# A retention layer with a token-mixing layer behind it: one product for wq and wk, explicit PSUM banks, late weights, a new order, 512-byte pieces and at most three loads on their way

## Chip, cores and metric

One core of one Trainium2 chip. The metric is the device time of the kernel in microseconds (us). A profile's span (first to last instruction) is 1.7 us shorter than the time of the same run. Runs of one kernel scatter: on the day of the experiments the kernel before ran from 108.9 to 118.0 us (on three chips), with the granted TensorE clock of a run between 0.92 and 0.98. A run counts as fast when it is within 1.5% of the fastest run of the same kernel.

## The reference, cut to what matters

```python
# retention: a recurrent state per batch and head, S = 768 steps, 8 heads of 64
state = gamma * state + outer(k[t], v[t]);   y[t] = scale * q[t] @ state
# token mixing on x = y of all heads side by side (4 batches x 768 x 512)
wq = x @ w_q;  wk = x @ w_k                              # 512 -> 64
W_tok = scale * einsum('bsd,btd->bst', wq, wk)
mixed = einsum('bst,btd->bsd', W_tok, x)
out = relu(mixed) @ w_out
```

The kernel works in 12 "pairs" of 256 tokens, three per batch. A pair needs 0.5 MB each of q, k and v. `mixed` is computed as wq times (wk^T x), so the mixing of a batch starts when its three pairs are through.

## The kernel before

Every instruction has its place in a hand-made list, `ORDER`: a token such as `sc.3.1` or `ekT.4:A` emits one step of one pair, the letter naming the engine (A ScalarE, V VectorE, P GpSimd). The engines work through their own instructions in that order.

```python
STAGES = 6
at_psum = pool("at_psum", 1, space=PSUM)   # scores: 2 banks, one buffer
y_psum  = pool("y_psum", 1, space=PSUM)    # 2 banks
s_psum  = pool("s_psum", 1, space=PSUM)    # 1 bank
psum    = pool("psum", 3, space=PSUM)      # everything else: 3 banks in turn

for p in range(STAGES):
    for name in "kqv":
        load(name, p)                      # k of pair 0 on ScalarE's queue, the rest on SyncE's
    if p == 2:                             # weights ahead of pair 3
        nc.sync.dma_start(out=wq_stage, in_=moe_w_q.rearrange("(a p) h -> p a h", p=128))
        nc.sync.dma_start(out=wk_stage, in_=moe_w_k.rearrange("(a p) h -> p a h", p=128))
        nc.sync.dma_start(out=wout_stage, in_=moe_w_out.rearrange("(a p) m -> p a m", p=128))
...
def wqk(e, p):                             # wq x transposed (wq doubled), wk x not
    for a in range(NDM):
        matmul(out=ps[:, 0:256], lhsT=wq_sb[:, a], rhs=xT[:, a])            # 4 of 256 columns
    for c in range(2):
        for a in range(NDM):
            matmul(out=ps[:, 256 + c*64 : ...], lhsT=xT[:, a, c], rhs=wk_sb[:, a])  # 8 of 64
def ew(e, p): copy(e, st["wqk"], st["wqk_ps"])                              # one copy of 384 columns
...
nc.sync.dma_start(out=dst, in_=pairs[p]["o"])                               # 4 KB a row
```
(cut and shortened to the parts that matter here)

Of the kernel before, what the change touches and what calls it, by code (L numbers as in the profile page):

```python
# [15 lines left out]

ORDER = """
fill.80 ck.0:V trk.0 cq.0:V ekT.0:A trq.0 cv.0:V fill.2 eqT.0:V
st.0 es.0.0:A sc.0.0 X.0 eat.0.0:V es.0.1:A sc.0.1 ck.1:P ia.0.0
eat.0.1:V cq.1:P Y.0 trk.1 fill.6 ekT.1:A ia.0.1 ex.0:V cv.1:P  # L20
trq.1 eqT.1:A xt.0 st.1 sc.1.0 exT.0:V ck.2:P es.1.0:A eat.1.0:V
X.1 es.1.1:A sc.1.1 cq.2:P trk.2 eat.1.1:V ia.1.0 ekT.2:V Y.1
ia.1.1 cv.2:A ex.1:V trq.2 st.2 fill.4 eqT.2:V xt.1 es.2.0:A
W:V sc.2.0 exT.1:A X.2 wqk.0 eat.2.0:V wqk.1 WO:A ew.0:V
sc.2.1 ew.1:V ia.2.0 eat.2.1:V ck.3:P Y.2 ia.2.1 ex.2:A cq.3:P
trk.3 xt.2 ekT.3:A fill.4 exT.2:V cv.3:A wqk.2 trq.3 ew.2:A
st.3 eqT.3:V zm.0 ck.4:P es.3.0:A ez.0:A X.3 sc.3.0 es.3.1:A
mx.0 eat.3.0:V r.0.1:A cq.4:P trk.4 r.0.0:A sc.3.1 ekT.4:A ia.3.0
eat.3.1:V mx.1 Y.3 r.1.0:A pj.0.0 cv.4:P r.1.1:A trq.4 fill.4
eo.0.0:A st.4 eqT.4:V ia.3.1 ck.5:P pj.0.1 ex.3:A es.4.0:V sc.4.0  # L30
eo.0.1:A X.4 eat.4.0:V xt.3 es.4.1:V cq.5:P trk.5 ekT.5:A exT.3:V
pj.1.0 sc.4.1 eo.1.0:A cv.5:P trq.5 eat.4.1:V ia.4.0 mx.2 eqT.5:A
YS.4 ia.4.1 es.5.0:A ck.6:P r.2.0:A ex.4:V wqk.3 trk.6 r.2.1:A
sc.5.0 pj.1.1 ew.3:A eat.5.0:V cq.6:P eo.1.1:A X.5 ekT.6:V ia.5.0
sc.5.1 cv.6:A xt.4 eat.5.1:V trq.6 pj.2.0 exT.4:A eqT.6:V ck.7:P
YS.5 eo.2.0:A sc.6.0 es.6.0:A ia.5.1 eat.6.0:V wqk.4 cq.7:P ex.5:A
pj.2.1 ew.4:A trk.7 eo.2.1:V xt.5 ekT.7:V sc.6.1 X.6 exT.5:V
cv.7:A eat.6.1:V trq.7 ia.6.0 eqT.7:A wqk.5 ck.8:P es.6.1:A sc.7.0
ew.5:V YS.6 eat.7.0:V es.7.0:A ia.6.1 zm.1 ex.6:A cq.8:P sc.7.1
ez.1:V X.7 eat.7.1:V trk.8 es.7.1:A xt.6 ekT.8:V cv.8:A ia.7.0  # L40
trq.8 exT.6:V Y.7 st.8 eqT.8:V mx.3 es.8.0:A ia.7.1 ck.9:P
r.3.1:A r.3.0:V sc.8.0 ex.7:V wqk.6 eat.8.0:V pj.3.0 ew.6:A cq.9:P
trk.9 eo.3.0:A pj.3.1 ekT.9:V X.8 eo.3.1:A cv.9:P mx.4 sc.8.1
r.4.0:A r.4.1:V trq.9 eat.8.1:V pj.4.0 eqT.9:A ck.10:P ia.8.0 eo.4.0:V
mx.5 YS.8 r.5.1:A r.5.0:V sc.9.0 ia.8.1 es.9.0:V pj.4.1 cq.10:P
ex.8:V trk.10 eo.4.1:A eat.9.0:V pj.5.0 ekT.10:A trq.10 cv.10:A eo.5.0:V
sc.9.1 X.9 eat.9.1:V ia.9.0 xt.8 ck.11:P xt.7 eqT.10:A exT.7:V
pj.5.1 exT.8:V wqk.7 es.9.1:V cq.11:P eo.5.1:A trk.11 ew.7:A wqk.8
YS.9 ew.8:V cv.11:P ekT.11:A sc.10.0 ia.9.1 es.10.0:A eat.10.0:V trq.11
ex.9:A zm.2 eqT.11:V X.10 ez.2:A sc.10.1 es.10.1:A ia.10.0 eat.10.1:V  # L50
mx.6 YS.10 r.6.0:A xt.9 es.11.0:A r.6.1:A sc.11.0 exT.9:V ia.10.1
mx.7 eat.11.0:V pj.6.0 r.7.0:A ex.10:V r.7.1:A wqk.9 eo.6.0:A pj.6.1
ew.9:A X.11 eo.6.1:A sc.11.1 ia.11.0 eat.11.1:V mx.8 pj.7.0 r.8.0:A
r.8.1:A Y.11 eo.7.0:V ia.11.1 pj.7.1 ex.11:A eo.7.1:A xt.10 xt.11
exT.10:V pj.8.0 exT.11:V wqk.10 eo.8.0:A wqk.11 ew.10:A pj.8.1 ew.11:A
zm.3 eo.8.1:A ez.3:A mx.9 r.9.0:A r.9.1:V mx.10 pj.9.0 r.10.1:A
r.10.0:V eo.9.0:V pj.9.1 mx.11 eo.9.1:A r.11.1:V r.11.0:A pj.10.0 eo.10.0:A
pj.10.1 eo.10.1:A pj.11.0 eo.11.0:A pj.11.1 eo.11.1:A
""".split()

STAGES = 6
# [3 lines left out]
def kernel(  # L65
# [10 lines left out]




# [3 lines left out]
    nc = tc.nc  # L83
# [20 lines left out]

# [3 lines left out]
    ost_pool = pool("ost", 7)  # L108
# [8 lines left out]
    moe_pool = pool("moe", 6)  # L117
    relu_pool = pool("relu", 2)
    PSUM = bass.MemoryType.PSUM
    at_psum = pool("at_psum", 1, space=PSUM)  # L120
    y_psum = pool("y_psum", 1, space=PSUM)
    s_psum = pool("s_psum", 1, space=PSUM)
    psum = pool("psum", 3, space=PSUM)

    pairs = [dict() for _ in range(NG)]
    state_ps = [None] * B
# [13 lines left out]
    def load(name, p):  # L140
        src = {"k": k, "q": q, "v": v}[name]
        b, cp = divmod(p, NP)
        t = stage_pool.tile([128, H, 2, D], FP32, name=name + "_st")
        eng = nc.scalar if (name, p) == ("k", 0) else nc.sync
        eng.dma_start(
            out=t.rearrange("g h j d -> g h (j d)"),
            in_=src[b, :, cp * 2 * C : (cp + 1) * 2 * C, :].rearrange(
                "h (g j) d -> g h (j d)", j=2
            ),
        )  # L150
        pairs[p][name + "_st"] = t

    wq_stage = wstage_pool.tile([128, NDM, DH], FP32, name="wq_stage")
    wk_stage = wstage_pool.tile([128, NDM, DH], FP32, name="wk_stage")
    wout_stage = wstage_pool.tile([128, NDM, DM], FP32, name="wout_stage")
    for p in range(STAGES):
        for name in "kqv":
            load(name, p)
        if p == 2:
            nc.sync.dma_start(out=wq_stage, in_=moe_w_q.rearrange("(a p) h -> p a h", p=128))  # L160
            nc.sync.dma_start(out=wk_stage, in_=moe_w_k.rearrange("(a p) h -> p a h", p=128))
            nc.sync.dma_start(
                out=wout_stage, in_=moe_w_out.rearrange("(a p) m -> p a m", p=128)
            )

    def release(name, p):

        if p + STAGES < NG:
            load(name, p + STAGES)



    warm = const_pool.tile([128, 128], BF16, name="warm")
# [23 lines left out]

# [20 lines left out]
    wq_sb = const_pool.tile([128, NDM, 2, DH], BF16, name="wq_sb")  # L218
    wk_sb = const_pool.tile([128, NDM, DH], BF16, name="wk_sb")
    wout_sb = const_pool.tile([128, NDM, DM], BF16, name="wout_sb")  # L220

    def W(e):
        copy(
            e,
            wq_sb,
            wq_stage[:, :, None, :].to_broadcast([128, NDM, 2, DH]),
        )
        if e == "A":
            nc.scalar.mul(out=wk_sb, in_=wk_stage, mul=float(wk_scale))
        else:  # L230
            ENGINES[e].tensor_scalar_mul(out=wk_sb, in0=wk_stage, scalar1=float(wk_scale))
# [4 lines left out]


    fills = [0]

    def filled(dst):  # L240
        for i in range(fills[0]):
            if dst.dtype == BF16:
                nc.tensor.transpose(dst, warm, identity)  # L243
            else:
                nc.tensor.matmul(out=dst, lhsT=warm, rhs=warm, start=True, stop=True)
        fills[0] = 0
# [3 lines left out]
    def decay(e, p, name, table):  # L250
        st = pairs[p]
        st[name + "s"] = cast_pool.tile([128, HP, 2, 2, D], BF16, name=name + "s")
        ENGINES[e].tensor_tensor(  # L253
            out=st[name + "s"].rearrange("p hp j x d -> p x (hp j) d"),
            in0=st[name + "_st"].rearrange("p (x hp) j d -> p x (hp j) d", x=2),
            in1=table[:, p % NP]
            .rearrange("p (x hp) j -> p x (hp j)", x=2)
            .to_broadcast([128, 2, HP * 2, D]),
            op=ALU.mult,
        )  # L260
        release(name, p)

    def ck(e, p):
        decay(e, p, "k", fk)

    def cq(e, p):
        decay(e, p, "q", fq)

    def cv(e, p):
        st = pairs[p]  # L270
        st["vs"] = cast_pool.tile([128, HP, 2, 2, D], BF16, name="vs")
        copy(
            e,
            st["vs"].rearrange("p hp j x d -> p x (hp j) d"),
            st["v_st"].rearrange("p (x hp) j d -> p x (hp j) d", x=2),
        )
        release("v", p)

    def trk(e, p):
        st = pairs[p]  # L280
        ps = psum.tile([128, HP, 2, 2, G], BF16, name="ktr_ps", tag="ps")
        filled(ps[:, 0, 0].rearrange("p c g -> p (c g)"))
        for hp in range(HP):
            for j in range(2):
                nc.tensor.transpose(ps[:, hp, j], st["ks"][:, hp, j], identity)  # L285
        st["ktr_ps"] = ps

    def ekT(e, p):
        st = pairs[p]
        st["kT"] = qkt_pool.tile([128, HP, 2, 2, G], BF16, name="kT")  # L290
        copy(e, st["kT"], st["ktr_ps"])

    def trq(e, p):
        st = pairs[p]
        ps = psum.tile([128, HP, 2, 2, G], BF16, name="qtr_ps", tag="ps")
        filled(ps[:, 0, 0].rearrange("p c g -> p (c g)"))
        for hp in range(HP):
            for j in range(2):
                nc.tensor.transpose(ps[:, hp, :, j, :], st["qs"][:, hp, j], identity)  # L299
        st["qtr_ps"] = ps  # L300

    def eqT(e, p):
        st = pairs[p]
        st["qT"] = qkt_pool.tile([128, HP, 2, C], BF16, name="qT")
        copy(e, st["qT"], st["qtr_ps"].rearrange("p hp c j g -> p hp c (j g)"))

    def sc(e, p, half):
        st = pairs[p]
        ps = at_psum.tile([128, 2, 2, 2, C], FP32, name="at_ps", tag="at")
        filled(ps[:, 0, 0, 0, :])  # L310
# [13 lines left out]
        st["at_ps", half] = ps  # L324

    def eat(e, p, half):
        st = pairs[p]
        st["at", half] = at_pool.tile([128, 2, 2, 2, C], BF16, name=f"at_sb{half}")
        st["eat", half] = ENGINES[e].tensor_tensor(  # L329
# [283 lines left out]
```

## Time and profile before

| | before |
|---|---|
| time, median | 112.4 us |
| span in the profile | 109.7 us |
| first useful TensorE instruction | 8.9 us |
| last matmul ends | 105.2 us |
| last load issued | 61.5 us |
| TensorE / VectorE / ScalarE / GpSimd busy | 93.8 / 64.9 / 60.0 / 49.4 us |

TensorE runs the matmuls and transposes, and is the busiest engine. The prediction below shows the slices, the stretches and the waits. To compare kernels I use one more number, the **work done** by a moment: the matmuls of every group that started before it, times their warm spacing (0.056 us a transpose or a 128-column product, 0.216 a 512-column projection and so on, from the chain and the fills). It counts neither fills (dummy matmuls, explained below) nor waits. Some matmul records are missing in a trace, so totals are 75 to 78 us; differences under 1 us mean nothing. It is to be compared only with itself: the prediction adds up whole groups and has 16.2 us by 36.1 us for the kernel before, this count has 14.9 by 36.

### The profile page before, as it was taken

Reading aid. Unit: us, or ns where it says so; the run is one execution under the profiler, and the core shown is the slowest. Engines: PE = TensorE matmul, PEld = TensorE weight load, DVE = VectorE, ACT = ScalarE, POOL = GpSimd, SP = SyncE. Lnnn points to the kernel's source line nnn. Section 1 sums busy time; section 2 is a strip of 40 time slices with the busy share of each in tenths; the row PEclk is TensorE's granted clock in tenths of the full one; section 3 lists DMA queues with packets and bytes.
Section 4 is the critical chain, followed back from the end, with each engine's and each line's share of the span. In section 5 each row is a group of like instructions: output and inputs, shape, how many; then the busy total and the mean of one; then the engine's idle time right before and its main releaser. Section 6 shows DMA issues by size and latency. Waiting matters only on the chain.

```text
span 109.7 us, 4707 instructions
## 1 busy us (share of the span) xinstructions
PE 93.8 (85%) x2132; PEld 68.9 (63%) x2132; DVE 64.9 (59%) x87; ACT 60.0 (55%) x94; POOL 49.4 (45%) x41
## 2 busy tenths in 40 slices
PE   3999596994579899999998959999999999958930
PEld 3998485783458576667687837557787647633400
DVE  1066756894422665687688849799857954225100
ACT  5004137265273975958848515549587866554640
POOL 6405968008699996968229999321000000000000
PEclk9999958999967999999999999999999999999999
DMA  1999999999999999999999999824040022430471
GB/s 38 309 347 346 342 342 238 313 334 306 289 327 337 345 344 304 339 337 333 287 297 281 300 354 370 332 115 166 31 197 0 6 87 111 191 158 33 191 312 73
DMA packets 40917, 26.77 MB, mean 244 GB/s; under 512 B 1857, under 2 KB 38721, under 8 KB 40897
## 3 DMA queue, kind: packets, MB, share of 16 engines
q1 hardware_dynamic: 39856, 25.96, 75.0%
q10 hardware_dynamic: 1040, 0.52, 1.6%
q8 instruction: 16, 0.26, 0.9%
q14 instruction: 5, 0.03, 0.1%
HBM read 20.19 MB, written 6.29 MB: 241 GB/s over the span
## 4 chain that ended last, share of the span: by engine, by line
PE 78%; DVE 10%; issue 5%; ACT 3%; POOL 1%; POOLq 0%; DVEq 0%; ACTq 0%
PE o_ps L538 20%; PE at_ps L316 8%; PE y_ps L422 6%; PE ktr_ps L243 6%; PE xt_ps L445 6%; DVE at_sb L329 6%; PE wqk_ps L460 6%; PE qtr_ps L299 6%; PE y_ps L385 5%; PE ktr_ps L285 3%; PE z_ps L492 3%; PE wqk_ps L470 3%; PE mx_ps L514 3%; PE state_ps L385 2%; DVE xT L133 1%
## 5 line engine op out<-in xcount | busy, mean ns | idle before, releaser
L329 DVE TENSOR_TENSOR at_sb<-at_ps,cmask 128x1024 bf16<-128x1024 f32 x24 | 29.3, 1222 | 9.5 <-PE at_ps L316 9.3
L253 POOL TENSOR_TENSOR ks<-k_st,fk 128x1024 bf16<-128x1024 f32 x11 | 20.9, 1902 | 19.0 <-DMA k_st<-in_k_dram 14.8
L538 PE MATMUL o_ps<-wout_sb,relu 128*128 128x512 bf16 x96 | 24.1, 380 | 0.3 <-ACT o_st L132 0.3
L253 POOL TENSOR_TENSOR qs<-q_st,fq 128x1024 bf16<-128x1024 f32 x11 | 20.9, 1902 | 1.2 <-DMA q_st<-in_q_dram 1.2
L132 ACT COPY o_st<-o_ps 128x512 f32<-128x512 f32 x19 | 11.1, 586 | 9.9 <-PE o_ps L538 9.8
L316 PE MATMUL at_ps<-qT,kT 64*64 64x128 bf16 x384 | 10.6, 221 | 4.0 <-DVE at_sb L329 2.3
L538 PEld LDWEIGHTS <-relu 128*128 128x128 bf16 x96 | 8.2, 98 | 8.0 <-issue 1.2
L132 ACT COPY kT<-ktr_ps 128x1024 bf16<-128x1024 bf16 x7 | 7.1, 1015 | 9.9 <-PE ktr_ps L285 9.9
L529 ACT ACTIVATE relu<-mx_ps 128x512 bf16<-128x512 f32 x18 | 10.2, 598 | 3.3 <-PE mx_ps L514 2.6
L316 PEld LDWEIGHTS <-kT 64*64 64x64 bf16 x384 | 7.1, 106 | 6.7 <-issue 5.6
L132 ACT CAST s_sb<-state_ps 128x256 bf16<-128x256 f32 x16 | 6.0, 373 | 8.8 <-PE state_ps L385 8.7
L385 PE MATMUL y_ps<-s_sb,qT 64*64 64x64 bf16 x320 | 9.6, 195 | 1.0 <-DVE at_sb L329 1.0
L133 DVE COPY xT<-xt_ps 128x1024 bf16<-128x1024 bf16 x10 | 6.7, 686 | 6.1 <-PE xt_ps L445 6.1
L385 PEld LDWEIGHTS <-qT 64*64 64x64 bf16 x320 | 7.2, 108 | 4.7 <-issue 2.7
L385 PE MATMUL state_ps<-vs,ks 64*64 64x64 bf16 x320 | 8.9, 194 | 1.5 <-issue 1.4
L422 PE MATMUL y_ps<-vs,at_sb 64*128 64x64 bf16 x384 | 10.0, 193 | 0.2
L243 PEld LDWEIGHTS <-warm 128*128 128x128 bf16 x90 | 7.7, 129 | 1.9 <-DVE warm L174 1.1
L422 PEld LDWEIGHTS <-at_sb 64*128 64x128 bf16 x384 | 7.2, 96 | 2.6 <-DVE at_sb L329 0.5
L132 ACT CAST x_nat<-y_ps 128x1024 bf16<-128x1024 f32 x6 | 6.1, 1012 | 4.7 <-PE y_ps L422 4.6
L243 PE MATMUL ktr_ps<-identity,warm 128*128 128x128 bf16 x80 | 7.0, 275 | 1.9 <-POOL identity masks.py:199 1.9
L385 PEld LDWEIGHTS <-ks 64*64 64x64 bf16 x320 | 6.9, 109 | 2.4 <-issue 2.1
L531 DVE TENSOR_SCALAR relu<-mx_ps 128x512 bf16<-128x512 f32 x6 | 4.2, 692 | 7.1 <-PE mx_ps L514 7.1
(57 smaller groups left out, 137.5 us busy)
## 6 DMA issues: line engine op xcount, KB each, us to landing
q_st<-in_q_dram SPq DMA_DIRECT2D x12, 512.0 KB, 6.7
v_st<-in_v_dram SPq DMA_DIRECT2D x12, 512.0 KB, 6.5
k_st<-in_k_dram SPq DMA_DIRECT2D x11, 512.0 KB, 6.7
out_dram<-o_st SPq DMA_DIRECT2D x11, 512.0 KB, 2.7
wout_stage<-in_moe_w_out_dram SPq DMA_DIRECT2D x1, 1024.0 KB, 7.0
k_st<-in_k_dram ACTq DMA_DIRECT2D x1, 512.0 KB, 5.6
out_dram<-o_st SPq DMA_DIRECT2D x2, 256.0 KB, 2.8
wq_stage<-in_moe_w_q_dram SPq DMA_DIRECT2D x1, 128.0 KB, 5.4
```

What stands on the lines that cost most here:

```text
L132: return nc.scalar.copy(out=out, in_=in_)
L133: return ENGINES[e].tensor_copy(out=out, in_=in_)
L243: nc.tensor.transpose(dst, warm, identity)
L253: ENGINES[e].tensor_tensor(out=st[name + "s"].rearrange("p hp j x d -> p x (hp j) d"), in0=st[name + "_st"].rearrange("p (x hp) j d -> p x ...
L299: nc.tensor.transpose(ps[:, hp, :, j, :], st["qs"][:, hp, j], identity)
L316: nc.tensor.matmul(out=ps[rows(c), x, hi, j, :], lhsT=st["kT"][rows(x), hp, j, c, :], rhs=st["qT"][rows(x), hp, c, :], start=(hi == 0 and ...
L329: st["eat", half] = ENGINES[e].tensor_tensor(out=st["at", half].rearrange("p x hi j t -> p (x hi) (j t)"), in0=st["at_ps", half].rearrange ...
L385: out.append(nc.tensor.matmul(skip_group_check=True, **mm))
L422: nc.tensor.matmul(out=st["y_ps"][:, c, x, hp, :], lhsT=st["at", half][rows(c), x, hi, j, :], rhs=st["vs"][rows(c), hp, j, x, :], start=(( ...
L445: nc.tensor.transpose(ps[:, a, c, :], st["x"][:, c, a * 128 : (a + 1) * 128], identity)
L529: nc.scalar.activation(out=dst, in_=src, func=ACT.Relu)
L538: nc.tensor.matmul(out=ps, lhsT=st["relu"][:, a, j], rhs=wout_sb[:, a, :], start=(a == 0), stop=(a == NDM - 1),)
```

## The change

Intent: less TensorE work, no wait of one step for another's bank, q, k and v of the first pairs before the big weights, short queues. The core of the diff:

```diff
-STAGES = 6                      # per kind
+LOADS = "q0 v0 k1 q1 v1 k2 q2 v2 w k3 q3 v3 k4 q4 v4 k5 q5 v5 o k6 q6 v6 ...".split()
+STAGES = 18                     # shared by q, k and v
...
+        if len(issued) >= 3:    # load n waits until load n-3 has landed
+            tc.add_manual_dep(dma.ins, issued[-3].ins.name, ...)
+        issued.append(dma)
...
+    load("k", 0, 0, nc.scalar)  # the first k in two halves, on two queues
+    load("k", 0, 1, nc.sync)
...
-    moe_w_q.rearrange("(a p) h -> p a h", p=128)          # rows of 256 B
+    moe_w_q.rearrange("(p a) h -> p a h", a=NDM)          # rows of 1 KB
-    at_psum, y_psum, s_psum, psum pools
+    banks = psum.tile([128, 8, 512], FP32, name="banks")  # every token names its bank: sc.0.0@0 X.0@2 sc.0.1@4
...
     def wqk(e, b, p):
-        4 matmuls of 256 columns, 8 of 64
+        for c in range(2):
+            for a in range(NDM):
+                matmul(out=ps[:, c, :], lhsT=xT[:, a, c, :], rhs=wqk_sb[:, a, :])   # 8 of 128
+    ewq: copy the wq half, doubled;  ew: copy the wk half
+    tw:  two transposes of the doubled wq half;  ewt: copy them
...
-    relu in two halves of 512 columns
+    relu in one instruction of 1024
...
-    nc.sync.dma_start(out=dst, in_=pairs[p]["o"])
+    nc.sync.dma_start(out=dst, in_=pairs[p]["o"], max_dma_last_dim=512)             # pieces of 512 B
```

`ORDER` is new as a whole. The opening fills (dummy matmuls, there to bring the TensorE clock up and keep it up) go from 80 of 128 columns to 20 of 512. No store is issued before the last load.

## The prediction

> **What bounds the kernel now.** I read the page first (busy shares, the slices), then the table by stretches, the waits between 9 and 36 us, the chain in order of time, and the timelines of TensorE and the load queue.
>
> From the page: shares of the span, then four rows of the 40 slices of 2.74 us.
>
> ```profile
> PE 93.8 (85%) x2132; PEld 68.9 (63%) x2132; DVE 64.9 (59%) x87; ACT 60.0 (55%) x94; POOL 49.4 (45%) x41
> ...
> PE   3999596994579899999998959999999999958930
> ...
> PEclk9999958999967999999999999999999999999999
> DMA  1999999999999999999999999824040022430471
> GB/s 38 309 347 346 342 342 238 313 334 306 289 327 337 345 344 304 339 337 333 287 297 281 300 354 370 332 115 166 31 197 0 6 87 111 191 158 33 191 312 73
> ```
>
> TensorE (PE) is the busiest engine, but not evenly: before slice 14 (38 us) there are holes and two slices of granted clock at 0.5 and 0.6; after it the row is nearly all nines. The DMA row is full until slice 25 (71 us). So there are two regimes: a load-fed one to about 36 us, a TensorE-bound one after it. The stretches say the same (busy us of each engine, clock, DMA share, GB/s):
>
> ```profile
> 9.00:18.00 9.00, 7.42 (x193) 6.25 (x191) 5.55 (x7) 4.05 (x6) 7.68 (x5) 0.81 1.12 320
> ...
> 27.00:36.00 9.00, 7.04 (x161) 5.73 (x160) 2.61 (x3) 4.09 (x6) 8.14 (x5) 0.81 1.08 320
> ...
> 72.00:81.00 9.00, 9.00 (x236) 6.81 (x236) 7.42 (x11) 5.93 (x8) 1.04 (x1) 1.00 0.25 98
> ```
>
> The waits of 9 to 36 us name the supplier, and one gap without a supplier:
>
> ```profile
> POOL ks L253 <- DMA k_st<-in_k_dram: 12.9, 4, 5.7
> ...
> PE at_ps L316 <- DVE at_sb L329: 1.9, 2, 1.1
> PE at_ps L316 <- issue: 1.4, 1, 1.4
> ```
>
> GpSimd waits up to 5.7 us for a k tile. Its timeline puts that wait at 18.8 to 24.6 us: the k tile of pair 3. The load queue's timeline shows why: the three weights (1.31 MB) were issued at 13.4 to 16.6 us, ahead of it. TensorE then has only pairs 0 to 2 to work on.
>
> A stretch of the chain (start, duration) gives warm costs per step:
>
> ```profile
> 46.64 0.54 PE wqk_ps L460 x4
> 47.18 0.23 PE wqk_ps L470 x8
> 47.41 0.52 PE ktr_ps L285 x8
> 47.93 0.35 PE at_ps L316 x16
> 48.28 0.97 PE o_ps L538 x4
> 49.25 0.37 PE y_ps L385 x16
> ```
>
> Each group is some 0.1 us longer where it follows one of another array tiling; elsewhere in the chain L460 x4 is 0.44, eight transposes 0.45, L538 x4 0.86. A pair then costs: k and q transposes 0.90, scores 0.70, attention times v 0.68, state and query-times-state 0.74, x transposes 0.45, wq/wk product 0.44+0.23 = 0.67, z 0.78/3 = 0.26, mixing 0.22, output projection 2x0.86 = 1.72: 6.34 us. Twelve pairs make 76.1; four lone state steps of 0.37 bring it to **77.6 us**. By 36.1 us the timeline shows done: 8 groups of transposes (3.6), 7 of scores (2.45), 6 of attention times v (2.0), 11 of state (4.0), 3 of x transposes (1.35), 3 of wq/wk (2.0), one z (0.8), together 16.2 us of work in the 27.2 us since the first useful transpose at 8.9. **Eleven are lost there.** The remaining 61.4 take 69.1, until the last matmul ends at 105.2: 7.7 lost, much of it changes of tiling and small gaps. Last copy and store take the 4.5 us to the end of the span. Reported time is 2.6 us above the span (112.3 against 109.7).
>
> **What the Trainium skill says.**
> - "TensorE: Matmul & The Clock Gate", section "Back-to-back issue gap": warm spacing N/2.4 + 2.5 ns, so 56 ns for N=128 and 109 for 256, with a floor of 25 ns for small N. The chain agrees: 0.45/8 = 56, 0.44/4 = 110, 0.23/8 = 29.
> - Same page, "What's actually happening": the clock is halved until activity has lasted about 3.4 us and after an idle window. The 80 opening fills took 7.0 us where 80x56 ns is 4.5, which agrees; of the two later slow slices I only see that they lie where TensorE has holes.
> - "DMA: Bandwidth & Descriptors", "Specifications": pieces under 512 B are below line rate. The trace has 1857 such packets; wq and wk are loaded in rows of 256 B (1024 packets), and slice 6, where the rate falls to 238 GB/s, lies just after their issue. That fits, but does not prove it.
> - "Runtime: NRT & Kernel Launch", "Instruction fetch mechanics": instructions are refilled in 16 KiB blocks by DMA, mostly hidden. The trace has 16 packets, 0.26 MB, on an instruction queue. TensorE's two "issue" gaps, 1.40 and 1.35 us, may be late refills; no view proves it.
>
> **The change, part by part.**
> *One product for wq and wk.* Removed per pair: 4 matmuls of 256 columns and 8 of 64 (0.67 us). Added: 8 of 128 (8x56 = 0.45) and 2 transposes (0.11). Net 0.11, over 12 pairs **-1.3 us**, all on TensorE. But evacuation grows: one copy of 384 columns (482 ns ACT, 555 DVE) becomes three (256, 128, 256 columns; some 0.3 to 0.4 us each), off TensorE's path, with one longer chain from product to mixing.
> *Relu in one instruction.* Two halves of 598 ns on ACT become one of 1024; the x_nat cast of that size takes 1012. A saving of 0.2 a pair, on an idle-enough engine: nothing.
> *DVE load.* From the operation order: 24 masks x1.222 = 29.3, 22 bf16 copies x0.686 = 15.1, decays and v casts 9.0, output copies 9x0.69 = 6.2, five relus x1.22 = 6.1, the rest about 12.5: an estimated 78 us against 64.9. ACT stays near 58. DVE at 78 of 100 isn't the bound on average.
> *Explicit banks.* Scores and y alternate over bank pairs, so the next scores need not wait for the mask of the last (2.3 us of TensorE waits in the whole span, 1.9 before 36 us).
> *Fills.* 90 of 128 columns become 32 of 512. The first 20 start without waiting for the identity (1.9 us): some 11 cold at 427 ns and 9 warm at 216 end near 8.0, **-0.9** against 8.9. Splitting the first k in halves has data ready before that.
> *Late weights.* Wout moves behind pair 5: 1.05 MB at 320 GB/s takes 3.3 us off k of pair 3; wider rows for wq and wk about 1 more (1.49+0.92 us to issue 0.26 MB, whose share at 1.45 us a load of 0.52 MB is 0.73). K3 lands near 20 instead of 24.6. By the new order TensorE then has pair 3 when it is through with pair 2. I take two thirds of the gap as recovered: the 11.0 lost become 4.5, **-6.5**.
> *Three loads on their way.* A load is issued when the third before it has landed. A lone 512 KB store needs 2.7 us from issue to landing; three loads at the present pace are 3x1.45 = 4.35 us. So the pipe should stay full, and landing (now 6.7) should drop to about 4.5 us without costing bandwidth: 0.
> *512-byte stores.* Twelve 0.5 MB outputs go from rows of 4 KB to eight times as many packets, the size the loads have. After 71 us DMA is below half busy; only the last store is on the path: 0 to +0.3, taken as 0.
> *New order later on.* 7.7 lost become about 7.2: **-0.5**.
> Sum: -1.3-0.9-6.5-0.5 = -9.2. Span 109.7-9.2 = 100.5; with 2.6 it is 103.1. Unseen stalls of a new order rather add than subtract, so **103.5 us**.
>
> **The rivals.**
> (a) *Early gap hidden by something else*: pair 0's chain (transpose, copy, scores, mask, product) is serial, and pairs 1 and 2 still arrive only every 4.6 us (1.57 MB at 345 GB/s). Then the clock falls again and only 2 to 3 us come back: 107 to 108. For it: the 0.5 slice lies at 14 us, before the weights matter. Against: later scores no longer wait for masks, and the largest hole is after 24 us.
> (b) *DVE becomes the bound*: it is at 7.3 to 7.4 of 9 us in some late stretches already; with 20% more it would hold masks and copies back. Some 106 to 109. Against: the rise is spread, and half the waits of DVE now are for TensorE.
> (c) *Load limit starves the pipe*: completion latency plus issue exceeding two queued loads. At 10% less bandwidth the 20.2 MB end near 68 us instead of 62; TensorE still has a backlog then, so 1 to 3 us, 105. Against: the 2.7 above.
> (d) *All holes close*, including the issue gaps because instruction refills meet shorter queues: another 3 to 4, 99 to 100.
>
> **Range and chances.** Central case and (c) at moderate effect make 101 to 105, (d) sets the low end 99.0, (a) with some of (b) the high end 108.0. To be within 2% (above 110.1), more than three quarters of the gain must vanish: both (a) and (b). Chances: faster 0.92, same 0.06, slower 0.02.
>
> **What would show it.** Right: first useful transpose near 8; the wait for k3 gone and its landing near 20; clock slices of 0.5 fewer; TensorE holes between 9 and 36 us of 4 to 5 us in place of 11; wq/wk plus transposes at 0.56 a pair; DVE busy near 78; load landing near 4.5 us with 320 to 350 GB/s kept. Wrong: long TensorE waits for DVE in the late stretches (b), GB/s under 310 while loading (c), a half-clock slice and holes between 9 and 20 us (a).

## The result

107.58 us (median of 4) against 112.43; ratio 0.957, interval 0.951 to 0.963. Ratios are the mean time of one kernel's fast runs over that of the other's of the same rounds, so not quite the ratio of the medians. A profile's span is 1.7 us shorter than the time of the same run. The forecast direction and range held, but the gain is 4.8 us where 8.9 were expected.

The page of the changed kernel, the lines that answer to those in the prediction:

```profile
PE 90.7 (85%) x2040; PEld 61.9 (58%) x2040; DVE 74.6 (70%) x108; ACT 54.5 (51%) x87; POOL 45.3 (43%) x41
...
PE   5997897899899859999996966999699999999800
...
PEclk9999999999999999999999998599999999999995
...
GB/s 28 318 236 347 348 326 308 323 298 316 333 303 301 327 285 314 287 324 280 319 319 242 273 325 228 286 347 342 204 89 117 0 178 26 198 174 30 337 346 111
```

A slice is 2.65 us; slices are counted from 1 here, from 0 in the prediction. In the first 13 slices no digit after the first is under 7, where the kernel before had 4s and 5s, and its two half-clock slices there are gone. But deeper holes now stand in slice 15 (37 to 40 us) and in slices 22, 24, 25 and 29 (56 to 77 us), and a half-clock slice is the 26th (66 to 69 us). Loading goes on until slice 28 (74 us). The same in stretches (busy us of each engine, granted clock, DMA share, GB/s):

```profile
9.00:18.00 9.00, 7.06 (x223) 4.87 (x223) 7.88 (x10) 4.96 (x7) 3.81 (x2) 1.00 1.14 340
27.00:36.00 9.00, 8.29 (x223) 6.42 (x221) 7.38 (x11) 4.97 (x10) 8.38 (x6) 1.00 1.07 313
36.00:45.00 9.00, 7.52 (x228) 5.23 (x226) 6.90 (x9) 5.29 (x8) 3.42 (x3) 1.00 1.04 300
63.00:72.00 9.00, 7.45 (x166) 5.22 (x166) 5.78 (x7) 4.21 (x6) 7.84 (x5) 0.81 1.00 290
72.00:81.00 9.00, 7.98 (x264) 6.34 (x258) 6.95 (x10) 5.08 (x11) 0.25 (x1) 1.00 0.69 205
```

The first column after the length is TensorE: 8.29 at 27 to 36 us where it was 7.04 at a lower clock; 7.52 and 7.98 at 36 and 72 us where it was 8.56 and 9.00. The chain that ended last says who holds it, first for the kernel before, then for the changed one:

```profile
PE 78%; DVE 10%; issue 5%; ACT 3%; POOL 1%; POOLq 0%; DVEq 0%; ACTq 0%
```
```profile
DMA 55%; PE 32%; SPq 3%; POOL 2%; issue 2%; ACT 1%; DVE 0%; POOLq 0%
```

Before, the chain followed back from the end stays on TensorE. Now it runs mostly along loads released by the third before them, until k of pair 10 has landed at 62.4 us. How much of it is loads changes from run to run: in the control, the same kernel once more, it reads

```profile
PE 53%; DMA 36%; issue 2%; DVE 1%; SPq 1%; ACT 1%
```

TensorE's own waits, from the changed kernel's list (total, times, longest):

```profile
PE banks L308 <- POOL ks L274: 3.0, 3, 1.9
PE banks L580 <- DVE wout_sb L127: 1.3, 1, 1.3
```

The first are k tiles that came late through GpSimd's cast, the second is wout. And the load queue's issues (KB each, median us from issue to landing), before and after:

```profile
k_st<-in_k_dram SPq DMA_DIRECT2D x11, 512.0 KB, 6.7
out_dram<-o_st SPq DMA_DIRECT2D x11, 512.0 KB, 2.7
...
out_dram<-o_st SPq DMA_DIRECT2D x2, 256.0 KB, 2.8
```
```profile
k_st<-in_k_dram SPq DMA_DIRECT2D x11, 512.0 KB, 5.2
out_dram<-o_st SPq DMA_DIRECT2D x11, 512.0 KB, 4.2
...
out_dram<-o_st SPq DMA_DIRECT2D x2, 256.0 KB, 3.3
```

Loads land sooner after issue, stores later. Three loads of 0.524 MB per 5.2 us are an estimated 302 GB/s. The last load is issued 4 us later than before but lands only 1.6 us later (70.6 against 69.0 us), because fewer are on their way ahead of it; k of pair 10 lands 3.5 us later (62.4 against 58.9). Counted as work done:

| kernel | by 36 us | 36 to 72 us | last load issued | last matmul ends | end of span |
|---|---|---|---|---|---|
| before | 14.9 | 31.3 | 61.5 | 105.2 | 109.7 |
| changed | 19.9 | 29.5 | 65.5 | 100.5 | 106.1 |
| changed, control run | 19.3 | 29.6 | 65.1 | 99.6 | 105.2 |

Five us more are done by 36 us, nearly two are given back until 72, and one at the end. In the kernel before TensorE is idle for 5.8 of the 27 us from 9 to 36 us, in the changed one for 3.2.

### The profile page after: what moved, and what is told of

The parts are those of the page before. It is cut to its first block, busy times and chain, and to the rows that moved or that the text cites. A ratio compares the mean times of both kernels' runs of the same rounds, so it can differ in the third digit from the quotient of the medians.

```text
span 106.1 us, 4558 instructions
## 1 busy us (share of the span) xinstructions
PE 90.7 (85%) x2040; PEld 61.9 (58%) x2040; DVE 74.6 (70%) x108; ACT 54.5 (51%) x87; POOL 45.3 (43%) x41
## 4 chain that ended last, share of the span: by engine, by line
DMA 55%; PE 32%; SPq 3%; POOL 2%; issue 2%; ACT 1%; DVE 0%; POOLq 0%
DMA k_st<-in_k_dram 47%; PE banks L580 15%; DMA v_st<-in_v_dram 8%; PE banks L474 2%; PE banks L447 2%; PE banks L410 2%; PE banks L558 2%; PE banks L488 2%; SPq L164 2%; POOL ks L274 2%; PE banks L536 1%; PE banks L323 1%; PE banks L344 1%; PE banks L308 1%; PE banks L514 1%
## 5 line engine op out<-in xcount | busy, mean ns | idle before, releaser
L356 DVE TENSOR_TENSOR at_sb<-banks,cmask 128x1024 bf16<-128x1024 f32 x24 | 28.8, 1219 | 5.2 <-PE banks L344 3.5
L580 PE MATMUL banks<-wout_sb,relu 128*128 128x512 bf16 x96 | 23.8, 389 | 1.5 <-DVE wout_sb L127 1.3
L274 POOL TENSOR_TENSOR ks<-k_st,fk 128x1024 bf16<-128x1024 f32 (+1 forms) x10 | 18.2, 1818 | 14.9 <-DMA k_st<-in_k_dram 11.1
L126 ACT CAST x_nat<-banks 128x1024 bf16<-128x1024 f32 x11 | 11.1, 1011 | 5.4 <-PE banks L410 3.9
L126 ACT COPY o_st<-banks 128x512 f32<-128x512 f32 x15 | 8.6, 589 | 9.4 <-PE banks L580 9.4
L262 PE MATMUL banks<-warm 128*128 128x512 bf16 x32 | 9.7, 433 | 1.4 <-DVE warm L201 1.2
L344 PE MATMUL banks<-qT,kT 64*64 64x128 bf16 x384 | 10.2, 223 | 0.0
L410 PE MATMUL banks<-s_sb,qT 64*64 64x64 bf16 x320 | 9.8, 195 | 0.0
L447 PE MATMUL banks<-vs,at_sb 64*128 64x64 bf16 x384 | 9.3, 195 | 0.6 <-DVE at_sb L356 0.5
L410 PE MATMUL banks<-vs,ks 64*64 64x64 bf16 x320 | 8.8, 194 | 0.7 <-DVE vs L127 0.5
```

What stands on the lines that cost most here:

```text
L126: return nc.scalar.copy(out=out, in_=in_)
L262: nc.tensor.matmul(out=bank32(b), lhsT=warm[:, 0:128], rhs=warm, start=True, stop=True)
L274: ENGINES[e].tensor_tensor(out=st[name + "s"][:, :, :, xs].rearrange("p hp j x d -> p x (hp j) d"), in0=st[name + "_st"][:, xs].rearrange( ...
L344: nc.tensor.matmul(out=ps[rows(c), x, hi, j, :], lhsT=st["kT"][rows(x), hp, j, c, :], rhs=st["qT"][rows(x), hp, c, :], start=(hi == 0 and ...
L356: ENGINES[e].tensor_tensor(out=st["at", half].rearrange("p x hi j t -> p (x hi) (j t)"), in0=st["at_ps", half].rearrange("p (xhi jt) -> p ...
L410: out.append(nc.tensor.matmul(skip_group_check=True, **mm))
```

## Experiments

Theory A: the new order and late weights gave the early gain, and the limit of three makes the loads the bound of the middle, with small stores costing the end. Rivals: the limit is free; the loads as such, not the limit, are the bound; the early hole was never a matter of loads.

All kernels were timed in five rounds beside the kernel before. The three batches ran on three chips (0, 7 and 13), and only the second has a control, so a comparison from one batch to another is one between chips too. This holds for every comparison with the control (106.82) or with a_noload (100.88) of a kernel outside the second batch.

| run | median of all (us) | range (us) | fast runs to fast runs of before |
|---|---|---|---|
| a_nolimit | 106.05 | 102.25-107.10 | (one fast run) |
| a_store4k | 106.41 | 105.33-107.69 | 0.957 [0.944, 0.970] |
| a_twoprod | 108.20 | 106.70-109.41 | 0.968 [0.949, 0.987] |
| b_limit3 | 112.88 | 110.70-114.20 | (two fast runs) |
| a_ctrl | 106.82 | 105.91-109.95 | 0.949 [0.942, 0.956] |
| a_both | 105.66 | 104.28-107.97 | 0.935 [0.925, 0.945] |
| a_noload | 100.88 | 100.78-101.21 | 0.899 [0.894, 0.905] |
| b_noload | 108.48 | 106.80-111.16 | 0.952 [0.944, 0.961] |
| a_earlyw | 109.71 | 108.39-111.73 | 0.996 [0.979, 1.013] |
| a_hybrid | 106.23 | 103.69-108.32 | 0.951 [0.911, 0.991] |
| a_hybrid_o4 | 107.17 | 105.38-110.45 | 0.969 [0.945, 0.993] |
| a_noload_two | 102.55 | 102.41-102.87 | 0.935 [0.926, 0.943] |

The medians of the kernel before were 113.08, 113.17 and 112.08 in the three batches (four kernels each, in the order of the table). In the first and third it had only two fast runs, and in the third they were quick (110.5 and 108.9), so ratios of the third batch read too high.

### a_nolimit: the limit taken out of the changed kernel

```diff
-        if len(issued) >= 3:
+        if len(issued) >= 10**6:
```

> The changed kernel with the wait of each load for the third before it taken out; up to eight loads are then on their way[...]. Theory A (the limit costs bandwidth: three loads of 0.52 MB that land 5.2 us after issue are 302 GB/s): the last load is issued near 61 us instead of 65.5, the loads move over 325 GB/s, TensorE's 1.9 us wait for a k tile and the half-clock slice at 66 us go, and the time falls from 107.6 to 103.5-105.5. Rival B (HBM or the DMA engines set the pace, the limit only takes queueing away): loads end within 1 us of 65.5 and the time stays 107-108.5; the issue gaps of TensorE may grow.

The last load is issued at 60.9 us, with a landing of 6.3 to 6.5 us. The load queue's last loads, changed kernel and then this one (start, duration of the issue):

```profile
65.48 0.37 SPq L147 DMA_DIRECT2D v_st<-in_v_dram  x1
```
```profile
60.92 2.41 SPq L147 DMA_DIRECT2D v_st<-in_v_dram  x1
```

So the limit does hold the loads back, by more than 4 us of issue and 2.7 us of landing (the last load lands at 67.9 against 70.6). Not eight but at most five loads are on their way at once, as in the kernel before. The median is 106.05 against 106.82 of the control one batch later: less than the expected 2 to 4 us, within the scatter of 102 to 107. Work by 18 us is 4.8 instead of 5.5, and the first useful transpose starts at 8.0 instead of 7.0. That late start is not the limit's doing. The 20 opening fills run one behind the other until it, and how many of them run at half clock (0.43 us apart instead of 0.216) differs from trace to trace. Changed kernel, this one, and a_store4k, which has the limit (start, duration):

```profile
1.24 5.88 PE L262 MATMUL banks<-warm 128*128 128x512 bf16 x20 [1.24 <-DVE warm L201]
```
```profile
1.24 6.88 PE L262 MATMUL banks<-warm 128*128 128x512 bf16 x20 [1.24 <-DVE warm L201]
```
```profile
1.24 6.90 PE L262 MATMUL banks<-warm 128*128 128x512 bf16 x20 [1.24 <-DVE warm L201]
```

The casts of the first k end at 6.0 and 6.2 us in the first two, ahead of the fills. In the eleven traces of kernels with these fills they speed up 2.9 to 6.0 us after the first of them, and the first useful transpose starts between 7.0 and 8.5 us; the earliest and the latest both have the limit. Neither Theory A's size nor the rival's "no effect on the loads" came true.

### b_limit3: the limit alone, in the kernel before

```diff
+        if len(issued) >= 3:
+            tc.add_manual_dep(dma.ins, issued[-3].ins.name, ...)
+        issued.append(dma)
```

> The kernel before with one part alone: each q, k, v load waits for the third before it. Theory A (the limit costs bandwidth): loads end 3 to 5 us later than in the kernel before, time 113.5-115.5 against 112.4. Rival B (the limit is free): 112-112.8. Rival C (the limit lets instruction refills and first tiles through sooner): issue gaps under 1 us and time 110.5-112.

Last load issued at 67.0 us (5.4 later), k of pair 3 ready for its cast at 27.8 us (3.2 later), and no time lost: 112.88 against 113.08, its two fast runs 110.7 and 110.85 against 110.16 and 111.57. TensorE's issue gaps add up to 3.1 us as before, so the limit does not shorten them either. **The kernel before had slack for later loads.** The size of the slack can be read in its trace: the cast of k of pair 3 ends at 26.5 us, and TensorE transposes that tile at 29.4, after waits for other things:

```profile
29.36 0.62 PE L285 MATMUL ktr_ps<-identity,ks 128*128 128x128 bf16 x8
```

With the tile 3.2 us later, TensorE's list has one wait for it, of 0.3 us. That speaks against the reading of its early hole in the prediction, and called for the next pair.

### a_noload and b_noload: no loads after pair 2, on purpose wrong

```diff
+        if p >= 3:
+            pairs[p][name + "_st"] = pairs[p - 3][name + "_st"]
+            return
```

> Wrong on purpose: the changed kernel with only the first three pairs loaded, every later pair working on the tiles of the pair three before it (same instructions on every compute engine, no load after 18 us but wout). Theory A (loads, paced by the limit, hold the changed kernel until 67 us): 5 to 8 us faster than the control, 100-102.5. Rival B (TensorE and its serial chains hold it): less than 2 us, 105.5-107.

> Wrong on purpose: the kernel before in the same way, loads of the first three pairs only. The prediction took its early hole for a wait for loads (11 us lost before 36 us, 6.5 of them to be had by earlier loads): then 106-108. Rival (a) of the prediction, the holes are serial chains of pair 0 to 2, which another load order doesn't touch, as the three-loads-limit on it, with k of pair 3 landing 3 us later and no time lost, suggests: 111-112.5.

The results are wrong. a_noload: 100.88, 5.9 below the control, with all runs within 0.4 us. b_noload: its fast runs 106.8 to 107.0 against 111.5 to 113.0, 5.3 less (three of its six runs are slow, at 109.9 to 111.2). That is in the range put down for the prediction's reading, 106 to 108, and outside the one for rival (a). So **loads cost both kernels 5 to 6 us**, and the difference between the kernels without loads is 6.0 us, no smaller than with them. But where they cost it is not where the prediction had it. TensorE's stretches of b_noload:

```profile
27.00:36.00 9.00, 6.47 (x172) 5.23 (x174) 3.52 (x4) 5.81 (x10) 6.96 (x5) 1.00 0.01 4
36.00:45.00 9.00, 9.00 (x246) 6.20 (x244) 5.81 (x8) 6.84 (x11) 6.03 (x5) 1.00 0.16 62
```

At 27 to 36 us no byte is missing any more (4 GB/s on the queues), and TensorE is still busy only 6.47 of 9 us. Its work by 36 us is 16.2 instead of 14.9. So the hole is not a wait for loads but the serial steps: product, copy, scores, mask, next product, one behind the other for too few pairs. TensorE's waits from 9 to 36 us in b_noload are all for masks, copies and a weight cast. What b_noload gains comes mostly after 36 us (34.6 instead of 31.3 by 72); the half-clock slices, which it does not have, lie before 36 us in the kernel before. From 36 to 72 us TensorE is idle for 2.2 us in the kernel before and for next to nothing in b_noload, and most of that is the **issue gaps, which vanish**: 3.1 us in the whole span of the kernel before, none of 0.2 us or more in TensorE's list of b_noload and a_noload. In the changed kernel they are 1.7 us.

The gaps are instruction refills. The packed traces hold every DMA packet, and among them 16 of 16 KB on an instruction queue (no view prints them one by one). In the fourteen traces TensorE has 28 issue gaps of 0.2 us or more, and every one of them ends 1.2 to 1.6 us after one of these packets has landed; by chance some 2 of the 28 would. And loads delay the packets: the third to eleventh start after 27 to 173 more TensorE instructions in the kernel before than in b_noload, and in the changed kernel, but for one, after 49 to 182 more than in a_noload; the last four, when loads are over, start within 24 of each other.

| kernel | work by 36 us | 36 to 72 us |
|---|---|---|
| before | 14.9 | 31.3 |
| b_noload | 16.2 | 34.6 |
| changed | 19.9 | 29.5 |
| a_noload | 20.7 | 34.2 |

Read across: the change brings 4.5 to 5 us by 36 us with loads or without. (Counted again, matmul by matmul, the first column is 15.5, 16.6, 20.1 and 21.4; the differences are within 0.4 us of these.) Up to 1.8 us of it is the earlier first transpose; the rest is the new order with its banks and what else changed with it, which no run takes apart. From 36 to 72 us the loads cost the changed kernel 4.7 us of work, the kernel before 3.3: being ahead, it meets the loads.

### a_earlyw: wout loaded ahead of pair 3 again

```diff
-LOADS = "... q2 v2 w k3 ... k5 q5 v5 o k6 ..."
+LOADS = "... q2 v2 w o k3 ... k5 q5 v5 k6 ..."
```

> The changed kernel with wout loaded after pair 2 again, as in the kernel before (1 MB ahead of pair 3 instead of behind pair 5). If the late weights bring what the prediction said, k of pair 3 lands some 3 us later and the time rises by 2 to 3 us over the control's 106.8: 109-110. If what TensorE does before 36 us is set by its order and not by loads, as the two kernels without loads suggest, the work done by 36 us falls by at most 2 us, TensorE's wait of 1.3 to 2.1 us for wout goes, and the time is within 1 us of 106.8.

Here the first expectation held: 109.71, 2.9 us above the control of the batch before (on the same chip a_hybrid and a_hybrid_o4, which have wout late, have 106.23 and 107.17). GpSimd's cast of k of pair 3 (start, duration, idle before it), kernel before, changed kernel, a_earlyw:

```profile
24.56 1.90 POOL L253 TENSOR_TENSOR ks<-k_st,fk 128x1024 bf16<-128x1024 f32 x1 [5.73 <-DMA k_st<-in_k_dram]
```
```profile
21.52 1.90 POOL L274 TENSOR_TENSOR ks<-k_st,fk 128x1024 bf16<-128x1024 f32 x1 [0.36 <-DMA k_st<-in_k_dram]
```
```profile
25.69 1.90 POOL L274 TENSOR_TENSOR ks<-k_st,fk 128x1024 bf16<-128x1024 f32 x1 [3.85 <-DMA k_st<-in_k_dram]
```

And TensorE's waits in a_earlyw:

```profile
PE banks L308 <- POOL ks L274: 4.4, 2, 3.5
PE banks L344 <- issue: 1.9, 1, 1.9
```

In the new order the late k tile reaches TensorE (3.5 us at one stroke, work by 36 us 15.9); in the old order GpSimd waited 5.7 us for it and TensorE's own list shows no wait for it. So late weights are worth some 3 us to an order that is ready for the tile. That they would bring the old order nothing is likely, since k of pair 3 had 2.9 us of slack there, but no run loads wout late in the old order. (The profile fell in a slow run; the waits are read as places, not to the tenth. Part of its 1.9 us issue gap may be scatter.)

### a_store4k: stores in rows of 4 KB again

```diff
-            nc.sync.dma_start(out=dst, in_=pairs[p]["o"], max_dma_last_dim=512)
+            nc.sync.dma_start(out=dst, in_=pairs[p]["o"])
```

> The changed kernel with its outputs stored in rows of 4 KB (2 KB for the last) again instead of pieces of 512 B. Theory A (small pieces slow the stores, 4.2 us to landing against 2.7): last matmul to end of span falls from 5.5 to about 4.5 us, time 106.5-107. Rival B (the end is longer because four stores pile up there): landing of the last stores stays over 3 us, time 107.3-107.9.

Last matmul to end of span: 4.6 us (100.2 to 104.8) instead of 5.6, as Theory A said. The last two stores and the slices' rates:

```profile
out_dram<-o_st SPq DMA_DIRECT2D x2, 256.0 KB, 2.4
```
```profile
GB/s 25 307 212 346 344 342 341 277 316 234 294 266 307 267 326 286 337 305 313 321 320 273 310 330 297 256 325 414 283 58 172 0 130 77 200 108 99 297 384 123
```

In slices where stores alone run, rows of 4 KB reach 384 GB/s (and 414 beside the last loads); pieces of 512 B stop at 346. The landing of 4.2 us against 2.7 that the expectation started from is another matter. The eleven stores of 512 KB take 3.5 us in this run, but in a_both, which has rows of 4 KB too, as long as in pieces:

```profile
out_dram<-o_st SPq DMA_DIRECT2D x11, 512.0 KB, 4.2
```

A store that runs alone takes about 3.0 us in pieces and 2.6 in rows; the rest of the 4.2 is stores that overlap each other. So Rival B's pile-up is there, though its sign, the last stores over 3 us, did not come. The median, 106.41, is 0.4 below the control of the next batch, too little against the scatter, but the end of the span shows the cost in each kernel: 5.6 us in the five profiles with small pieces and all loads (changed, a_ctrl, a_nolimit, a_twoprod, a_earlyw), 4.6 to 5.0 in the four with rows of 4 KB (a_store4k, a_both, a_hybrid, a_hybrid_o4).

### a_twoprod and a_noload_two: wq and wk as two products again

```diff
-        8 matmuls of 128 columns; ewq, tw, ewt
+        4 matmuls of 256 columns (doubled wq), 8 of 64; ewq copies the transposed wq x; tw and ewt empty
```

> The changed kernel with wq and wk as two products again (4 matmuls of 256 columns with doubled wq, 8 of 64; no transpose of wq x, one evacuation less). TensorE gets 1.3 us more work over twelve pairs. If TensorE sets the time wherever loads do not, 108.3-109.0. If the loads set the time until 67 us, only the pairs after that count (about 5 of 12): 107.9-108.3. If evacuation by DVE matters more than TensorE time, it is faster: below 107.3.

> Wrong on purpose: the changed kernel without loads after pair 2 (100.88 us, runs within 0.4 us), with wq and wk as two products. Here TensorE is busy 89% of the span and no load hides a change: the prediction's 1.3 us for the product should show nearly in full, 101.8-102.4. If the added evacuations eat it, 100.5-101.2.

108.20 against 106.82, but with scatter of 2.7 us: it fits the prediction and proves little. Without loads the runs are within 0.5 us and the answer is clearer: 102.55 against 100.88, **1.7 us**, though on two chips. The chain of the changed kernel shows the new pieces (start, duration):

```profile
78.85 0.45 PE banks L488 x8
...
81.84 0.11 PE banks L514 x2
```

0.45 + 0.11 per pair as predicted, 1.3 us in twelve pairs. The other 0.4 us need not be the product: the profile of a_noload_two has a refill gap of 0.4 us, of which a_noload has none, and its first useful transpose is 0.2 us later. Evacuation did not eat the gain, though VectorE has 1.3 us more to do in a_noload (75.3 against 74.0).

### a_ctrl, a_both, a_hybrid, a_hybrid_o4: the control and tries for better

a_ctrl is the changed kernel again. a_both joins a_nolimit and a_store4k. a_hybrid keeps the limit for the first ten loads:

```diff
-        if len(issued) >= 3:
+        if 3 <= len(issued) < 10:
```
and a_hybrid_o4 also moves `o` ahead of `k5`.

> The changed kernel itself once more, as the control of this batch: 107-108, ratio to the kernel before 0.95-0.96. The last batch had more scatter (the kernel before from 110 to 117), so its differences under 1 us are read only against this one.

> The changed kernel without the wait for the third load before and with stores in rows of 4 KB: the two parts that alone gave 106.05 and 106.41. If they add (loads end 3 us earlier, last stores land 0.9 us earlier), 1.0-2.0 us below the control: 105-106.5. If the loads are no longer what TensorE waits for, only the stores' 0.9 us remain.

> A version meant to be better: the limit of three holds for the first ten loads only (without it the first useful transpose came near 8.0 us and 0.7 us less work was done by 18 us), then none; stores in rows of 4 KB. If the limit's harm is bandwidth after the start and its use is the start, this is 0.5-1.0 us below the kernel without any limit (105.66): 104.5-105.3. If the start does not matter: 105.3-106.

> The same with wout one pair earlier, behind pair 4. TensorE's wait of 1.3 to 2.1 us for wout at 38 us should go; pairs 5 and later land 0 to 3 us later at that place and equally late after pair 6. If TensorE has a backlog there, 0.5-1.5 us below the last one: 103.5-104.8; if it does not, the same.

a_both is below the control of its own batch by 1.2 us in the medians and 1.5 in the means of fast runs (105.0 against 106.5); their intervals against the kernel before overlap a little, so it is probably better, by about 1%. Its work from 36 to 72 us is 31.6 instead of 29.6. a_hybrid has the best profile (span 102.0, first useful transpose at 7.0, last load at 61.7), but its runs go from 103.7 to 108.3 and the median, 106.23, misses its expectation: whether it beats a_both is open. Its idea, that the limit brings the early start, was mistaken: a_hybrid_o4 has the same limit on the first ten loads and starts at 7.9. a_hybrid_o4 missed too, with 107.17: in its profile the wait for wout fell to 0.5 us, but TensorE then waited 2.6 us for a k tile. There the megabyte of wout only changed who waits.

## Why the prediction was partly right

It said 103.5; 107.6 was measured, inside the range and near its upper end. In the span it expected 109.7 - 9.2 = 100.5, and the profile has 106.1. Step by step:

- **First useful transpose near 8.0**: 7.0 (7.2 in the control), and the 1 us to the good is luck. The sum took 11 of the 20 fills at half clock; 7 were in this trace, 7 to 14 in the others. In the kernel before the clock came up 5.1 us after the first fill, not the 3.4 that the prediction quotes; in the other traces it took 2.9 to 6.0. (The kernel before has 100 fills in all, not 90.)
- **One product, -1.3**: right in mechanism and nearly in size, 1.7 us where no load interferes, of which the chain shows 1.3.
- **Late weights, k of pair 3 near 20 us, -6.5**: the tile came at 21.4 and the gain of 5 us more work by 36 us, start included, stands against the 7.4 forecast. The failing step is the inference that the 11 us lost before 36 us were a wait for loads. The line quoted for it was GpSimd's wait. TensorE's own waits in that stretch, two of which stand below it, were for masks and copies and for an instruction refill, never for k (1.9 and 1.0 us for VectorE's masking, 1.4 us of issue, the rest 0.6 or less). These are 5.5 of the 5.8 us that TensorE is idle there; the rest of the 11 is left for half clock, fills and changes of tiling, which nobody measured apart. Rival (a) named this, and b_noload shows it: without any later loads the old order does only 1.3 us more by 36 us. The gain was real because order and load order changed together, and that its size came near is partly luck; a_earlyw shows that the late weights are worth some 3 us inside the new order.
- **Three loads on their way, 0**: mis-sized. It took 2.7 us, the landing of a lone store, as the time that three loads at 1.45 us each have to cover, and expected a landing of 4.5 us. With two loads ahead of it a load needed 5.2 us, so three loads give 302 GB/s, and the last load is issued 4 us later and lands 1.6 us later. This is rival (c), with its sign of under 310 GB/s; it had the loads end at 68 us instead of 62 where the last issue moved from 61.5 to 65.5. What it costs in time is less sure: about 0.8 us in the pairs a_nolimit to control and a_both to a_store4k, both of them across two chips and neither clear of the scatter.
- **The bound after 36 us**: the prediction took TensorE to be the bound there whatever came, and put down -0.5. Instead the kernel that was 5 us ahead met the loads: 29.5 us of work from 36 to 72 where the kernel before did 31.3, and a_noload 34.2. Of the 5.6 us of span that are missing this is about 2.
- **512-byte stores, 0**: mis-sized, +0.6 to 1.0 at the end of the span.
- **Time above span, 2.6**: wrong by 0.9. A median was set against one profile, which must have come from a faster run; in every run it is 1.7 to 1.8. By this the forecast time was 0.9 us too long, which hid a part of the other errors.
- **DVE at 78 of 100 is no bound**: 74.6 measured, and no long wait of TensorE for VectorE except the late wout. Rival (b) did not come.
- **Rival (d), the issue gaps**: 1.7 us left of 3.1, and 0.8 to 3.6 in the other kernels with all loads. They close, but for 0.4 us in one trace, only without the later loads. That they are refills was right; the prediction held it only possible.

Together: 2.4 us short by 36 us, about 2 from 36 us to the last matmul, 1.0 at the end, near the 5.6 missed in the span.

## What to carry to other kernels

A wait in a feeding engine is not a wait of the bound: read the bound's own list of waits before giving a hole to a supplier, and, if it matters, run the kernel with that supplier's work removed. When a change gets the bound engine ahead, ask what it will run into next; here the loads, whose tiles had slack before, became the chain of the profiled run. A limit on loads in flight has to be sized with the landing time under load (three tiles per 5.2 us), not with that of a lone transfer.

## What the Trainium skill lacked or had wrong

- "DMA: Bandwidth & Descriptors", Specifications: gives 512 B as the size from which line rate is reached. For stores the runs differ: slices with stores alone reach 346 GB/s in 512 B pieces and 384 GB/s in rows of 4 KB, and the last two stores of 256 KB land in 3.3 against 2.4 to 2.8 us.
- The same page has no figure for how many half-megabyte loads on one queue are needed in flight: three land in 5.2 us each (302 GB/s, last load issued at 65.5 us), with no limit at most five are on their way and land in 6.4 us (last load issued at 60.9 us).
- "Runtime: NRT & Kernel Launch", Instruction fetch mechanics: calls the cost of a refill mostly hidden. TensorE's gaps without another visible cause are 3.1 us (before) and 1.7 us (changed) while data loads run, and at most 0.4 us in the three kernels whose later loads were removed. All 28 such gaps of 0.2 us or more in the fourteen traces end 1.2 to 1.6 us after a 16 KB instruction packet has landed. The page lacks that heavy loads delay the refills, and what that costs.
- No page says how far run-to-run times of one single-core kernel scatter: 108.9 to 118.0 us for the kernel before on one chip. Without later loads the changed kernel kept to 100.8 to 101.2 us, but the kernel before still ran from 106.8 to 111.2.
